# A gated mix of linear attention and a GLU block: the denominators' loads on another issuing queue, and the first weights of the second half loaded in pieces

## The chip, the cores and the metric

The kernel runs on one core of one Trainium2 chip. The metric is the time of one execution on the device, in microseconds (us), measured without the profiler. Beside these times there is one execution recorded by the hardware profiler: its trace gives the start and the length of every instruction on every engine, and of every DMA. The engines are TensorE (PE: matmuls; PEld: its weight loads), VectorE (DVE), ScalarE (ACT), GpSimd (POOL) and SyncE (SP). The last two issue DMAs in this kernel, each in the order of its own queue.

## The reference

The input is x with 2048 tokens (S) of 640 numbers (D), all in float32. There are two branches and a gate between them:

```python
q, k, v = split_heads(x @ wqkv)                   # 32 heads of 20
phi = lambda t: where(t > 0, t + 1, exp(t)) + 1e-6
pq, pk = phi(q), phi(k)
kv  = einsum("bhsd,bhse->bhde", pk, v)
z   = einsum("bhsd->bhd", pk)
num = einsum("bhqd,bhde->bhqe", pq, kv)
den = einsum("bhqd,bhd->bhq", pq, z)[..., None] + 1e-6
a   = merge_heads(num / den) @ wo
b   = (sigmoid(x @ w_gate) * (x @ w_up)) @ w_down   # F = 1536
g   = sigmoid((x * gate_w).sum(-1))
out = g * a + (1 - g) * b
```

The change touches `den`, the denominators: for each token and head, 20 products of `pq` with `z`, summed up; and the weights of the first GLU block (`w_gate`, `w_up`) in the second half of the tokens.

## The kernel before

**Matmuls.** Every product in float32 is computed as three matmuls of rounded parts (high by high, high by low, low by high; `mm3`, lines 404, 405 and 406, so a group of matmuls has one of these three lines in the profile). The large products use a scheme with seven block products in place of eight; class `Block` holds it, with steps `s1` to `s7`. Its operands are linear combinations of weight blocks (the *forms*, three per block: `wg`, `wu` and `ws`; they are computed once, stored to DRAM, and loaded again for the second half by `load_form`, line 1210) and of token blocks. Accumulators in PSUM are called `ch`, `cc`, `dd` and `rot`; VectorE and ScalarE read them (`c<-cc`, `tb<-rot`, `dd<-ch`) before TensorE may write on into the bank. In the profile the names mean: `hf` the gated product h and its rounding parts, `tb` the sum of the down projection, `mr` and `mt` the linear combinations of token sums on their way from and to DRAM (`m_dram`, `mp_dram`), `qe` and `qr` the values of phi(q), stored to `p_dram`.

**Stages.** The tokens lie in four groups of 512, and these in two pairs. The kernel first computes k, v and the sums, then for pair 1 (groups 2 and 3) the queries (`q_phase(1)`), then its 12 GLU blocks with the down projection (`f_phase(1)`, up to about 397 us), then the same for pair 0 (groups 0 and 1): `q_phase(0)`, about 409 to 444 us, and `f_phase(0)`, from about 434 to about 650 us, and at the end the attention's output and the mix. So "the second pair" in time is pair 0.

**q_phase (line 1942)** runs two blocks, A (query rows 2 and 3 of the five) and B (rows 0 and 1), and one plain row between, by a written list `steps`. Its last entries differ between the pairs. When A passes steps 2, 6 and 7 in pair 0, `load_form` is called for forms of the first blocks: after (A, 6) form 1, `wu`, of GLU block 0, and after (A, 7) its form 2, `ws` (2 by 1152 numbers on each of 128 partitions, 1152 KB). A `ws` tile has one of two buffers, and the load waits until the buffer's last reader is done.

**The denominators (`queue_dens`, line 1397)** are queued twice in `f_phase(0)`: at GLU block 3 for groups 2 and 3, at block 7 for groups 0 and 1. For each group they go in this order:

1. `load`: five tiles `pden` (128 partitions by 512, 256 KB) are loaded from `p_dram`. There are four buffers ("t" tiles, shared with `qe` and `qr`): the loads of u = 0 and 1 of both groups go out first, and each further load when `one` has read the buffer before it.
2. `one`: VectorE multiplies a tile by a column of z (`zcol`) and adds it to `fac`. The first has one form (line 432, with `zeps`), the other four another (line 425).
3. `den_dram[:, g] <- fac`, a store on GpSimd's queue.
4. `turn_in`: four loads of 64 KB bring it back turned, `fac <- den_dram`, and one more brings `gs`, the gate.
5. `factor`: VectorE adds the four quarters, takes the reciprocal, multiplies with the gate; the result is stored to `fac_dram` by GpSimd.
6. `turn_out`: four loads `fac <- fac_dram` on SP's queue.

**Queues.** `sp` and `gp` are thin wrappers (`Ring`, with the one `dma_start` at line 361 that all DMA rows of the profile name) around SP's and GpSimd's queues. An issuing instruction waits in its queue until its tile is free, and those behind it wait with it. On SP's queue go most loads, on GpSimd's queue the stores and some loads.

**The planner.** VectorE's and ScalarE's work is not placed by hand. Class `Order` (lines 36 to 301) keeps estimated clocks of TensorE, VectorE and ScalarE while the program is written out, and sets each queued piece of work between the matmuls where the estimate has room and its data are due. It also estimates when a DMA lands (`order.when`), with an issue cost and a lag for each queue (SP: 0.38 and 1.5; GpSimd: 0.55 and 2.2, in the planner's microseconds). So a DMA that changes its queue can also change the static order of the instructions on VectorE and ScalarE.

Of the kernel before, what the change touches and what calls it, by code (L numbers as in the profile page):

```python
# [14 lines left out]
P = 128  # L15
# [352 lines left out]
def v_cost(w):  # L368
    return 0.07 + w / 960

@with_exitstack
def gated_mix_kernel(ctx: ExitStack, tc: tile.TileContext, xt, xn, wk, wv, wo, wst_q, wst_f, out_t):
# [8 lines left out]
    sp, gp = Ring(nc.sync, order, rings, 0, 0.38, 1.5), Ring(nc.gpsimd, order, rings, 1, 0.55, 2.2)  # L381

    def f32(ap):
        return ap.bitcast(F32)
# [34 lines left out]
    def vec2(out, a, b, op, after=""):  # L419
        order.on_vec(width(out), after, 1.0, out, a, b)  # L420
        nc.vector.tensor_tensor(out, a, b, op=op)  # L421

    def vec3(out, a, scalar, b, op0, op1, after=""):
        order.on_vec(width(out), after, 1.0, out, a, b)
        nc.vector.scalar_tensor_tensor(out, a, scalar, b, op0=op0, op1=op1)

    def vec1(out, a, s0, s1=None, op0=OP.mult, op1=None, after=""):
        order.on_vec(width(out), after, 1.0, out, a)
        if op1 is None:
            nc.vector.tensor_scalar(out, a, s0, None, op0=op0)  # L430
        else:
            nc.vector.tensor_scalar(out, a, s0, s1, op0=op0, op1=op1)
# [10 lines left out]
    def add(out, a, b, after=""):  # L443
        vec2(out, a, b, OP.add, after)
# [10 lines left out]
    fac = common.tile([P, NG, TG], F32, name="fac")  # L455
    p_dram = dram.tile([P, KC, NG, TG], F32, name="p_dram")
# [260 lines left out]
    w_dram = {}  # L717
# [249 lines left out]
    c0 = chunks[0]  # L967
# [51 lines left out]
    g = GTBatch(0, [0])  # L1019
# [8 lines left out]
    for c in range(1, 4):  # L1028
        ck = chunks[c]
        if c == 1:  # L1030
# [14 lines left out]
            g = GTBatch(c, batches[c])  # L1045
# [59 lines left out]
        if c == 3:  # L1105
# [19 lines left out]
            def put(n, i, t):  # L1125
                WT[n, i] = t
                W[n, i] = [t[:, c] for c in range(2)]
# [15 lines left out]
        if c > 1:  # L1143
            g = GTBatch(c, batches[c])
# [50 lines left out]
    def tt(name, dt=F32, shape=(P, TG)):  # L1195
        return pw.tile(list(shape), dt, name=name, tag="t", bufs=4)
# [12 lines left out]

    def load_form(n, i):  # L1210
        t = (wg_tile, wu_tile, ws_tile)[i]()
        sp.dma_start(f32(t), w_dram[n[::2] + (i,)])
        put(n, i, t)

    entries = [("q", 1, 0)] + [("f", 1, f) for f in range(FC)]
# [136 lines left out]
    def phi_q(g, u, src, after="p"):  # L1352

        e = tt("qe")
        act(e, src, AF.Exp, after)
        r = src if after == "v" else tt("qr")
        act(r, src, AF.Relu)

        def rest():
            vec3(e, e, 1.0, r, OP.min, OP.add)  # L1360
            gp.dma_start(p_dram[:, u, g], e)
        order.need("phi")
        order.follow(v_cost(TG), rest, "phi")
# [33 lines left out]
    def queue_dens(*gs2):  # L1397

        st = {}

        def load(g, u):
            if u < KC:
                st[g, u] = tt("pden")
                sp.dma_start(st[g, u], p_dram[:, u, g])
                st["at", g, u] = lambda: order.when(st[g, u])

        def one(g, u):
            td = fac[:, g]
            if u == 0:
                vec1(td, st[g, u], zcol[:, 0:1], zeps[:, 0:1], OP.mult, OP.add)  # L1410
            else:
                vec3(td, st[g, u], zcol[:, u:u + 1], td, OP.mult, OP.add)
            load(g, u + 2)
            if u == KC - 1:
                gp.dma_start(den_dram[:, g], td)
                st["at", g, u + 1] = lambda: order.when(den_dram[:, g])

        def turn_in(g):
            for j in range(4):
                js = slice(j * H, (j + 1) * H)  # L1420
                sp.dma_start(fac[js, g].rearrange("h (d c) -> h d c", c=P),
                                  den_dram[:, g, j * P:(j + 1) * P].rearrange("(d h) c -> h d c", h=H))
            st[g, "gs"] = tt("gs")[:, :P]
            sp.dma_start(st[g, "gs"], gate_rep[4 * g:4 * g + 4].rearrange("i h c -> (i h) c"))
            st["at", g, KC + 1] = lambda: max(order.when(fac[:, g]), order.when(st[g, "gs"]))

        def factor(g):
            td = fac[:, g]
            q = td[:, :P]
            add(td[:, :2 * P], td[:, :2 * P], td[:, 2 * P:])  # L1430
            add(q, q, td[:, P:2 * P])
            order.on_vec(5 * P, "")
            nc.vector.reciprocal(q, q)
            vec2(q, q, st[g, "gs"], OP.mult)
            gp.dma_start(fac_dram[:, g], q)
            st["at", g, KC + 2] = lambda: order.when(fac_dram[:, g])

        def turn_out(g):
            for d in range(4):
                sp.dma_start(fac[d * H:(d + 1) * H, g].rearrange("h (j c) -> h j c", c=P),  # L1440
                                  fac_dram[:, g].rearrange("(j h) c -> h j c", h=H))
        order.add(0, 0, lambda: [load(g, u) for u in range(2) for g in gs2], chain=True)
        for u in range(KC):
            for g in gs2:
                order.add(0, v_cost(TG), lambda g=g, u=u: one(g, u), None, lambda g=g, u=u: st["at", g, u](), chain=True)
        for n, (v, fn) in enumerate(((0, turn_in), (2.0, factor), (0, turn_out))):
            for g in gs2:
                order.add(0, v, lambda g=g, fn=fn: fn(g), ("fac", g) if n == 2 else None,
                          lambda g=g, n=n: st["at", g, KC + n](), chain=True)
# [492 lines left out]
    def q_phase(pr, b12, extra):  # L1942

        A, B = (Block(("q", pr, u)) for u in (2, 0))
        steps = [(A, 1), (A, 2)]
        steps += [(4, b) for b in range(2)]
        steps += [(B, 1), (B, 2), (A, 3), (A, 4)]
        steps += ([(A, 5), (A, 6), (A, 7), (B, 3), (B, 4), (B, 5)] if pr else
                  [(B, 3), (A, 5), (B, 4), (A, 6), (B, 5), (A, 7)]) + [(B, 6), (B, 7)]
        order.slack(True)  # L1950
        late = None
        for j, (u, b) in enumerate(steps):
            if isinstance(u, Block):
                blk, s = u, b
                if pr and u is B:
                    for k, key in ((1, ("wg", B.n)), (3, ("w", B.n, 0)), (4, ("w", B.n, 1))):
                        if s == k:
                            order.need(key)
                if s > 1:
                    order.need((nx[1], s if s < 7 else 2))  # L1960
                else:
                    order.need((nx[1], 2))
                getattr(blk, f"s{s}")()
                v = blk.n[2]
                if s == 3:
                    phi_q(2 * pr, v, blk.c11, "v")
                elif s == 6:
                    phi_q(2 * pr + 1, v + 1, blk.c22, "v")
                    phi_q(2 * pr, v + 1, blk.ch)
                elif s == 7 and blk is A:  # L1970
                    late = (2 * pr + 1, v, blk.c12, "v")
                elif s == 7 and pr:
                    phi_q(2 * pr + 1, v, blk.c12, "v")
                if late and blk is B:
                    phi_q(*late)
                    late = None
                if pr:
                    if blk is A and s == 2:
                        queue_g(B.n)
                        queue_s(B.n, 0, 1)  # L1980
                        queue_both(nx, 3)
                        queue_s(B.n, 1)
                    elif blk is A and s == 3:
                        queue_g(("f", pr, 0))
                    elif blk is A and s == 6:
                        load_w()
                    elif blk is A and s == 7:
                        queue_s(("f", pr, 0))
                else:
                    n = {2: ((A, "q", 0, 0), (B, "f", 1, 0)), 6: ((A, "f", 0, 1), (B, "f", 1, 1)),  # L1990
                         7: ((A, "f", 0, 2), (B, "f", 1, 2))}
                    for k, kind, f, i in n.get(s, ()):
                        if k is blk:
                            load_form((kind, 0, f), i)
            else:
                order.need((nx[1], "plain" if b else 2))
                q_unit(pr, u, b, b12)
                if b and not pr:
                    load_form(("f", 0, 0), 0)
            for fn in extra.get(j, ()):  # L2000
                fn()
            order.fill()
            if not pr and u is B and b > 4:
                yield
        if not pr:
            phi_q(2 * pr + 1, 0, B.c12, "v")
        order.slack(False)
# [599 lines left out]
```

## Time and profile before

| | us |
|---|---|
| times of three executions | 733.25, 735.68, 734.04 |
| their median | 734.04 |
| the profiled execution | 734.86 |
| its span, first to last instruction | 733.0 |
| TensorE busy in the span | 726.5 (99%) |
| VectorE busy | 561.6 (77%) |
| ScalarE busy | 355.4 (48%) |
| GpSimd busy | 94.5 (13%) |

How to read the rows that follow. In the *timeline* a row gives the start in us from the start of the span, the length, the engine, the line of the kernel, the operation, the written and the read tile, the shape, and how many such instructions in a row; brackets hold the engine's idle time just before it and what ended that. A DMA row on SPq or POOL is the issuing instruction, and its length there may contain the time that it waited. A row "DMA to landing" gives the times from issue to landing of a group of DMAs (least, median, largest). A row of the *windows* view begins with a stretch A:B, its length, and then the busy time and the number of instructions of the engines PE, PEld, DVE, ACT and POOL (where one engine was asked for, of that engine alone), the granted clock of TensorE as a share of full speed, the mean share of the DMA engines that was busy, and the GB/s moved. In the *waits* a row names an instruction that waited, what it waited for, and three numbers: the sum of the waiting, the count, and the longest. The *chain* follows the work that ended last back to the start; its rows give start, length and what it was.

### The profile page before, as it was taken

What the parts mean: (1) busy time and instruction counts of PE and PEld (TensorE: products, weight loads), DVE (VectorE), ACT (ScalarE), POOL (GpSimd) and SP (SyncE); (2) the same over time, 40 slices, a digit from 0 to 9 for tenths busy, and PEclk for the clock granted to TensorE, in tenths of its full rate; (3) what the DMA queues carried; (4) which work ended last, traced back from release to release, by engine and by line L of the source; (5) the groups of instructions that cost most, each with busy time, mean ns of one, the idle gap of its engine ahead of it and who ended that gap; (6) DMA issues with size and microseconds to landing.
All of it is one profiled execution on the core that took longest, in us unless ns stands there. A gap on an engine that the chain in (4) does not pass through costs nothing.

```text
span 733.0 us, 10098 instructions
## 1 busy us (share of the span) xinstructions
PE 726.5 (99%) x3575; PEld 622.3 (85%) x3575; DVE 561.6 (77%) x987; ACT 355.4 (48%) x661; POOL 94.5 (13%) x161
## 2 busy tenths in 40 slices
PE   9999999999999999999999999999999999999998
PEld 7999999988788888888888888887888888888886
DVE  4978777987677889898989942546685867699976
ACT  5765648358557653535355364453423232332541
POOL 0211111113211211211211211001000041000000
PEclk9999999999999999999999999999999999999999
DMA  8564648697877866557687558888889697859212
GB/s 262 133 195 109 187 120 248 149 343 272 299 276 259 330 239 234 190 213 256 256 328 265 215 175 300 305 244 297 272 278 345 196 335 207 308 209 371 81 68 102
DMA packets 71001, 173.54 MB, mean 237 GB/s; under 512 B 11642, under 2 KB 32394, under 8 KB 67238
## 3 DMA queue, kind: packets, MB, share of 16 engines
q1 hardware_dynamic: 54582, 109.99, 45.8%
q0 software_dynamic: 16224, 62.74, 24.0%
q8 instruction: 28, 0.46, 0.2%
q14 instruction: 23, 0.19, 0.1%
q10 hardware_dynamic: 144, 0.16, 0.1%
HBM read 103.96 MB, written 63.92 MB: 229 GB/s over the span
## 4 chain that ended last, share of the span: by engine, by line
PE 93%; DMA 2%; issue 2%; DVE 1%; ACT 1%; POOL 1%; SPq 0%; POOLq 0%; DVEq 0%; ACTq 0%
PE ch L404 10%; PE ch L406 10%; PE ch L405 10%; PE cc L404 8%; PE cc L406 8%; PE cc L405 8%; PE dd L404 7%; PE dd L405 7%; PE dd L406 7%; PE rot L404 6%; PE rot L405 6%; PE rot L406 6%; DMA pden<-p_dram 1%; DMA p_dram<-qe 1%; PE rot L1521 1%
## 5 line engine op out<-in xcount | busy, mean ns | idle before, releaser
L417 ACT ACTIVATE c<-ch 128x512 f32<-128x512 f32 x52 | 31.0, 597 | 88.1 <-PE ch L406 87.9
L421 DVE TENSOR_TENSOR hf<-c,hf 128x512 fp32r<-128x512 f32 x75 | 51.1, 687 | 25.9 <-ACT hf L417 25.5
L421 DVE TENSOR_TENSOR c<-cc,c 128x512 f32<-128x512 f32 x40 | 27.6, 690 | 40.7 <-PE cc L406 27.9
L417 ACT ACTIVATE hf<-c 128x512 fp32r<-128x512 f32 x75 | 46.0, 624 | 25.4 <-DVE c L421 25.4
L404 PE MATMUL ch<-xth,ws 128*128 128x512 f32 x112 | 43.9, 392 | 0.0
L405 PE MATMUL ch<-xtl,ws 128*128 128x512 f32 x112 | 43.6, 389 | 0.0
L406 PE MATMUL ch<-xth,ws 128*128 128x512 f32 x112 | 43.6, 389 | 0.0
L421 DVE TENSOR_TENSOR tb<-rot,tb 128x512 f32<-128x512 f32 (+1 forms) x61 | 39.3, 674 | 3.0 <-PE rot L406 3.0
L421 DVE TENSOR_TENSOR tb<-dd,tb 128x512 f32<-128x512 f32 x44 | 30.2, 686 | 8.7 <-PE dd L406 8.7
L404 PE MATMUL dd<-xrh,wg 128*128 128x512 f32 x90 | 35.2, 391 | 0.0
L406 PE MATMUL dd<-xrh,wg 128*128 128x512 f32 x90 | 35.0, 389 | 0.0
L405 PE MATMUL dd<-xrl,wg 128*128 128x512 f32 x90 | 35.0, 389 | 0.0
L417 ACT ACTIVATE c<-dd 128x512 f32<-128x512 f32 x22 | 13.2, 598 | 43.3 <-PE dd L406 43.3
L421 DVE TENSOR_TENSOR c<-c,c 128x512 f32<-128x512 f32 x46 | 31.6, 688 | 2.6 <-ACT c L417 2.0
L404 PE MATMUL cc<-xbh,ws 128*128 128x512 f32 x84 | 32.7, 389 | 0.0
L405 PE MATMUL cc<-xbl,ws 128*128 128x512 f32 x84 | 32.7, 389 | 0.0
L406 PE MATMUL cc<-xbh,ws 128*128 128x512 f32 x84 | 32.7, 389 | 0.0
L417 ACT ACTIVATE dd<-ch 128x512 f32<-128x512 f32 x22 | 12.8, 582 | 33.6 <-PE ch L406 33.6
L421 DVE TENSOR_TENSOR wst<-wst 128x256 f32<-128x256 f32 (+2 forms) x69 | 27.4, 413 | 1.5
L404 PE MATMUL rot<-pkh,xnh 128*128 128x320 f32 x90 | 28.0, 312 | 0.1
L405 PE MATMUL rot<-pkl,xnh 128*128 128x320 f32 x90 | 27.8, 309 | 0.0
L406 PE MATMUL rot<-pkh,xnl 128*128 128x320 f32 x90 | 27.8, 309 | 0.0
(648 smaller groups left out, 2325.7 us busy)
## 6 DMA issues: line engine op xcount, KB each, us to landing
wf<-ws POOLq DMA_DIRECT2D x12, 1152.0 KB, 7.6
ws<-wf SPq DMA_DIRECT2D x12, 1152.0 KB, 7.0
wst<-wst_f SPq DMA_DIRECT2D x12, 640.0 KB, 5.2
wf<-wg POOLq DMA_DIRECT2D x12, 640.0 KB, 6.4
wd<-wd POOLq DMA_DIRECT2D x12, 640.0 KB, 7.9
wg<-wf SPq DMA_DIRECT2D x12, 640.0 KB, 6.7
wf<-wd SPq DMA_DIRECT2D x10, 640.0 KB, 10.4
xnst<-xn SPq DMA_DIRECT2D x16, 320.0 KB, 4.2
```

What stands on the lines that cost most here:

```text
L404: nc.tensor.matmul(out, l_hi, r_hi, start=first, stop=False, skip_group_check=True)
L405: nc.tensor.matmul(out, l_hi, r_lo, start=False, stop=False, skip_group_check=True)
L406: nc.tensor.matmul(out, l_lo, r_hi, start=False, stop=last, skip_group_check=True)
L417: nc.scalar.activation(out, src, fn, **kw)
L421: nc.vector.tensor_tensor(out, a, b, op=op)
L1521: nc.tensor.matmul(ps[:w, :w], v[:, m, :w], gt[:, m, c0:c0 + w], start=(m == 0), stop=(m == KC - 1))
```

## The change

There are three edits.

1. The five `pden` loads of each group are issued by GpSimd's queue and not by SP's.
2. The four turning loads `fac <- den_dram` of each group are issued by GpSimd's queue and not by SP's.
3. For GLU block 0 of pair 0, form 2 (`ws`) is loaded in four pieces of columns, in the order 0 to 255, 896 to 1151, 640 to 895, 256 to 639; and in `q_phase(0)` the steps of the blocks A and B stand in another order: A's steps 5, 6 and 7 come each a place or two sooner, B's steps 3, 4 and 5 correspondingly later. The calls of `load_form` that hang on A's steps 6 and 7 move with them.

No arithmetic is added or removed.

```diff
     def load_form(n, i):
         t = (wg_tile, wu_tile, ws_tile)[i]()
-        sp.dma_start(f32(t), w_dram[n[::2] + (i,)])
+        w = t.shape[2]
+        for c0, c1 in ((0, 2 * P), (7 * P, w), (5 * P, 7 * P), (2 * P, 5 * P)) if n == ("f", 0, 0) and i == 2 else ((0, w),):
+            sp.dma_start(f32(t[:, :, c0:c1]), w_dram[n[::2] + (i,)][:, :, c0:c1])
         put(n, i, t)
...
         def load(g, u):
             if u < KC:
                 st[g, u] = tt("pden")
-                sp.dma_start(st[g, u], p_dram[:, u, g])
+                gp.dma_start(st[g, u], p_dram[:, u, g])
                 st["at", g, u] = lambda: order.when(st[g, u])
...
         def turn_in(g):
             for j in range(4):
                 js = slice(j * H, (j + 1) * H)
-                sp.dma_start(fac[js, g].rearrange("h (d c) -> h d c", c=P),
+                gp.dma_start(fac[js, g].rearrange("h (d c) -> h d c", c=P),
                                   den_dram[:, g, j * P:(j + 1) * P].rearrange("(d h) c -> h d c", h=H))
...
         steps += ([(A, 5), (A, 6), (A, 7), (B, 3), (B, 4), (B, 5)] if pr else
-                  [(B, 3), (A, 5), (B, 4), (A, 6), (B, 5), (A, 7)]) + [(B, 6), (B, 7)]
+                  [(A, 5), (B, 3), (A, 6), (A, 7), (B, 4), (B, 5)]) + [(B, 6), (B, 7)]
```

## Prediction

> **What bounds the kernel now.** I read the page first, then TensorE's waits, then the chain of work around the one wait that remains, and last the rows of VectorE and of the two issuing queues there. The times shown are 733.25, 735.68 and 734.04 us; the profiled execution took 734.86 us, 0.82 above their median, with a span of 733.0.
>
> ```profile
> span 733.0 us, 10098 instructions
> PE 726.5 (99%) x3575; PEld 622.3 (85%) x3575; DVE 561.6 (77%) x987; ACT 355.4 (48%) x661; POOL 94.5 (13%) x161
> ...
> PE 93%; DMA 2%; issue 2%; DVE 1%; ACT 1%; POOL 1%; SPq 0%; POOLq 0%; DVEq 0%; ACTq 0%
> ```
>
> TensorE is busy 99% of the span, so a change that adds and removes no matmul can win only what TensorE idles. After the first 400 us (from where the change acts) there is one idle time:
>
> ```profile
> PE rot L404 <- DVE tb L421: 1.4, 1, 1.4
> ```
>
> It stands in the timeline of TensorE, where a 512-column matmul follows the one before by 0.23 us:
>
> ```profile
> 494.57 0.39 PE L406 MATMUL rot<-hf,wf 128*128 128x512 f32 x1
> ...
> 496.61 0.39 PE L406 MATMUL dd<-hf,wf 128*128 128x512 f32 x1
> 498.41 0.50 PE L404 MATMUL rot<-hf,wf 128*128 128x512 f32 x1 [1.41 <-DVE tb L421]
> 498.75 0.39 PE L405 MATMUL rot<-hf,wf 128*128 128x512 f32 x1
> ```
>
> From 496.61 to 498.41 is 1.80 instead of 0.23: 1.57 us lost, and the restart costs 0.34 instead of 0.23: 0.11. The matmul writes on into a `rot` bank that VectorE must first read. The bank was complete about 494.6 to 495 (row 494.57), but VectorE came to it at 497.67:
>
> ```profile
> 480.71 0.69 DVE L421 TENSOR_TENSOR c<-cc,c 128x512 f32<-128x512 f32 x1 [2.89 <-PE cc L406]
> 483.27 0.69 DVE L421 TENSOR_TENSOR hf<-c,hf 128x512 fp32r<-128x512 f32 x1 [1.87 <-ACT hf L417]
> 486.56 1.29 DVE L421 TENSOR_TENSOR hf<-c,hf 128x512 fp32r<-128x512 f32 x2
> 490.03 1.21 DVE L432 TENSOR_SCALAR fac<-pden,zcol,zeps 128x512 f32<-128x512 f32 x2 [2.18 <-DMA pden<-p_dram]
> 491.44 1.42 DVE L425 SCALAR_TENSOR_TENSOR fac<-pden,zcol,fac 128x512 f32<-128x512 f32 x2 [0.20 <-DMA pden<-p_dram]
> ...
> 492.77 0.82 DVE L421 TENSOR_TENSOR mt<-mr,mt 128x640 fp32r<-128x640 f32 x1
> ...
> 497.00 0.75 DVE L425 SCALAR_TENSOR_TENSOR fac<-pden,zcol,fac 128x512 f32<-128x512 f32 x1 [0.61 <-DMA pden<-p_dram]
> 497.67 1.28 DVE L421 TENSOR_TENSOR tb<-rot,tb 128x512 f32<-128x512 f32 x2
> ```
>
> VectorE ran dry before 490.03 (2.18 us, for the first load of the denominators, `pden`) and before 497.00 (0.61). The chain names the same loads:
>
> ```profile
> 484.55 6.78 DMA pden<-p_dram
> ...
> 492.88 4.03 DMA pden<-p_dram
> ```
>
> They are late because of where they stand in SP's queue: behind the weights and the four pieces of `mr`, issued at 481.20, while GpSimd's queue has issued nothing since 448.15 (in the last row, 450 to 480, POOL is the fifth engine: 0.00 (x0)):
>
> ```profile
> 481.20 2.17 SPq L361 DMA_DIRECT2D mr<-m_dram  x4
> 483.54 9.65 SPq L361 DMA_DIRECT2D pden<-p_dram  x8
> 448.15 0.54 POOL L361 DMA_DIRECT2D p_dram<-qe  x1 [4.41 <-DVE qe L425]
> 450.00:480.00 30.00, 30.00 (x134) 24.86 (x133) 12.16 (x19) 9.65 (x17) 0.00 (x0) 1.00 0.72 264
> ```
>
> **Part 1, the `pden` loads on GpSimd's queue.** Twenty loads of 256 KB change queue; an issue costs GpSimd 0.54 (row 448.15) instead of SP's third of a microsecond. In the built program they follow the ten stores `p_dram<-qe` directly, so the first four (there are four buffers) leave soon after those stores have landed, some 30 us before they are used. With that the planner also sets VectorE's first two denominator steps earlier: behind the step of 480.71, before the `hf` of 483.27. I lay VectorE's new order on the rows. The first pair takes 1.21 and ends at about 482.5. `hf` stays at 483.27. The second pair takes 1.42 and ends at 485.3. The two `hf` of 486.56 end at 487.85. Then stand the third and fourth pairs, `mt`, one `c`, the fifth pair, and then the `tb` that TensorE waits for. Each load from the third pair on needs a buffer that VectorE has just left, so all depends on the time L from issue to landing on GpSimd's queue. These rows bound it: first all twenty `pden` loads on SP; then the GpSimd stores of the same size issued while 1152 KB of weights are in flight (438 to 449 us); last the `pden` loads of 489.5 to 494.
>
> ```profile
> DMA to landing us min/median/max: 2.6/4.6/8.0
> DMA to landing us min/median/max: 4.6/5.6/6.6
> DMA to landing us min/median/max: 2.6/2.9/3.3
> ```
>
> So L lies between 2.6 and 8.0. I take 5.6, from the same queue and size beside the same weight load. The last load of the third pair has its buffer at 482.5 and lands at 488.1, before it is wanted; VectorE ends that pair at 487.85 + 1.42 = 489.3. The fourth pair's buffers are free at about 484.6 and 485.3, so it lands at 490.2 and 490.9 and is done at 491.65. The fifth pair's last load starts there, lands at 494.9, and is used by 494.9 + 0.75 = 495.65. TensorE resumed 0.74 after its `tb` began (498.41 less 497.67), and would have gone on at 496.84 (496.61 + 0.23): a `tb` that begins by 496.10 costs no wait, and 495.65 does. So up to L = 6.05 the whole stall goes: 1.57 + 0.11 = 1.68 us. Above that both landings count: the `tb` begins at 482.5 + L + 0.75 + L + 0.75, so 484.0 + 2L, and equals the old 497.67 at L = 6.84. At 8.0 it begins at 500.0, 2.33 us worse than now.
>
> [...]
>
> What GpSimd delays: behind its waiting `pden` loads stand only stores of `mt` and of the denominators. What comes late next is the chain of `mr`, `mt` and its store, since ScalarE waits in it, in order, before freeing a `ch` bank:
>
> ```profile
> 508.26 0.74 ACT L417 ACTIVATE mt<-mr 128x640 fp32r<-128x640 f32 x1 [2.80 <-DMA mr<-m_dram]
> 508.91 0.58 ACT L417 ACTIVATE c<-ch 128x512 f32<-128x512 f32 x1
> ...
> 510.11 0.39 PE L404 MATMUL ch<-xth,ws 128*128 128x512 f32 x1
> ```
>
> TensorE reaches that bank at 510.11, and at 508.5 once the stall is gone; the bank is free at 508.91 + 0.58 = 509.5. `mt` would have to start about 1 us sooner. In VectorE's new order the first `mt` comes at 491.65 instead of 492.77, and the second waits for the `tb` steps, which come 2 us earlier (495.65 against 497.67). So I expect 1.1 to 2 us, and no new wait; if the chain did not move, 1.0 of the 1.68 would come back here.
>
> **Part 2, the turning.** Sixteen loads of 64 KB from `den_dram` also go to GpSimd. SP held them for long:
>
> ```profile
> 514.82 9.63 SPq L361 DMA_DIRECT2D fac<-den_dram  x4
> ```
>
> The weights queued behind them come up to those 9.6 us earlier, and no matmul waited for them: worth nothing. The factors that follow move up on VectorE, between the steps of 517.1 and 521.7. One factor fills 1.97 us (first row); the place has 4.61 - 0.69 = 3.92 free (second), and two need 3.94:
>
> ```profile
> 534.18:536.15 1.97, 1.87 (x5) 1.00 0.99 414
> 517.09:521.70 4.61, 0.69 (x1) 1.00 1.04 386
> ```
>
> So that costs nothing; without that cover up to 3.9 us of VectorE would stand before the next `c`. The stores behind the turning wait for VectorE anyway. `mt<-m_dram` and the like, 16 issues, go back by some 25 us behind the second factors; they have until 697.5:
>
> ```profile
> L421 DVE TENSOR_TENSOR mt<-mt x5: 284/419/425, 697.5 to 700.1; 128x256 f32<-128x256 f32 x4, 128x128 f32<-128x128 f32 x1
> ```
>
> **Part 3, the pieces of `ws` and the order of steps.** The diff also puts the second product block's third step behind the first block's fifth. The same matmuls run, the first block ends 4.9 us sooner and its `ws` buffer with it, so the load issued at 437.86 starts at about 433; three issues of 0.32 us are added. TensorE takes the load's first columns at 443.79, and it landed 5.4 us after its issue, at 443.26. It was in time by 0.5 us; earlier is worth nothing in this execution. One restart goes, 0.32 instead of 0.23, since that `ch` bank is now free long before:
>
> ```profile
> 437.86 0.32 SPq L361 DMA_DIRECT2D ws<-wf  x1
> DMA to landing us min/median/max: 5.4/5.4/5.4
> 434.15 0.48 PE L404 MATMUL ch<-xah,wg 128*128 128x512 f32 x1
> 434.47 0.39 PE L405 MATMUL ch<-xal,wg 128*128 128x512 f32 x1
> 443.79 0.39 PE L404 MATMUL ch<-xth,ws 128*128 128x512 f32 x1
> ```
>
> Added waits here: the fifth and sixth steps add onto a bank that ScalarE has just read, but a 1.36 us step of the other block now stands between, so I count 0; the reads take 0.6.
>
> **Sum.** 1.68 + 0.10 = 1.78 us of the profiled 734.86: 733.1. Taken from the median instead, 732.3. I forecast **732.5 us**, nearer to the median, which is what gets measured. A measurement of this kernel can tell about 0.3% from no change, 2.2 us; the whole gain that the profile offers is below that.
>
> **Rivals.** (a) *GpSimd's loads come late* (slower). L over 6.84, in both pairs that wait for a landing. For it: SP's own `pden` loads reached 8.0, and the second round falls into a stretch with as much traffic. Against it: 2.9 is the median once the weights have landed. At 8.0 the first round loses 2.33. In the second round a denominator step stands ahead of a `tb` of 563.38; its buffer is free one step of 0.54 after the `c` of 555.88, at about 557.1; the load lands at 565.1, and with 0.75 and the two `hf` (1.29) the `tb` begins at 567.1 and ends at 567.8, where TensorE wants the bank at 567.26:
>
> ```profile
> 555.88 0.69 DVE L421 TENSOR_TENSOR c<-cc,c 128x512 f32<-128x512 f32 x1 [2.95 <-PE cc L406]
> ...
> 563.38 0.69 DVE L421 TENSOR_TENSOR tb<-dd,tb 128x512 f32<-128x512 f32 x1 [0.92 <-PE dd L406]
> 567.26 0.39 PE L404 MATMUL dd<-hf,wf 128*128 128x512 f32 x1
> ```
>
> That is 0.6 more: 734.0 + 2.9 = **736.9 us**. (b) *Nothing is won*: L near 6.8, or the `mt` chain takes the place of the wait: 734.0 us, between 733.4 and 736. [...] (c) *More is won*: the executions without a profile lose more than this one, for instance where the `ws` of 437.86 lands over 0.5 us later; they spread over 2.4 us. Some 3 us less, **731.2 us**.
>
> **How the numbers follow.** The forecast, 0.47: 731.9 to 733.4 (the profiled base of 733.1 and 0.3 for the `mt` chain). (b) 0.14, (a) 0.22, (c) 0.17. Faster by over 0.3% (under 731.8) is (c), 0.17; slower (over 736.2) is (a), 0.22; the rest, 0.61, lies within. The range goes from 731.0, just beyond (c), to 736.9, the worst bound of L.
>
> **What would show it.** Right: no wait of TensorE for `tb` near 497; first `pden` issues on GpSimd at 449 to 455; the first denominator step at about 481.3; `ws` in four pieces from about 433. Wrong: a wait for `tb` that remains or grows, with VectorE idle for `pden` just before it (L over 6); a wait for the `ch` bank near 508 with ScalarE idle for `mr`; a wait for `dd` near 567; TensorE idle in the reordered block, 426 to 440. The forecast fails if landings on GpSimd's queue are much slower than its stores were.

## The result

The changed kernel takes **735.65 us** in the median of 20 executions (734.75 to 737.53), the kernel before 734.02 (733.25 to 737.2, 20 executions). The ratio, which compares all executions and not the two medians, is 1.0016 with a 95% interval of 1.0010 to 1.0023: 1.2 us slower (0.7 to 1.7). That is clear of zero and inside the 2.2 us that the prediction set as the bound of "the same". The time lies in the range of 731.0 to 736.9, but the forecast of 732.5 had the wrong sign.

The profiled execution of the changed kernel took 734.77 us, among the shortest of its 20. First its page and its waits of TensorE between 420 and 690 us (sum, count, longest):

```profile
span 733.0 us, 10118 instructions
PE 726.8 (99%) x3575; PEld 622.9 (85%) x3575; DVE 561.7 (77%) x987; ACT 355.1 (48%) x661; POOL 113.9 (16%) x197
...
PE rot L404 <- DVE tb L421: 1.0, 1, 1.0
```

The busy time is the same within 0.3 us, and one wait of TensorE for `tb` is still there. It is another one. Near 497 TensorE now goes through; the wait is near 567, in the second round of the denominators. The timeline of TensorE, of VectorE, and of GpSimd's queue there, and the landing of the four loads issued from 555.9 to 559.3:

```profile
567.12 0.40 PE L406 MATMUL cc<-hf,wf 128*128 128x512 f32 x1
568.49 0.47 PE L404 MATMUL rot<-hf,wf 128*128 128x512 f32 x1 [0.97 <-DVE tb L421]
...
555.09 0.99 DVE L432 TENSOR_SCALAR fac<-pden,zcol,zeps 128x512 f32<-128x512 f32 x2
...
562.74 0.75 DVE L425 SCALAR_TENSOR_TENSOR fac<-pden,zcol,fac 128x512 f32<-128x512 f32 x1 [2.53 <-DMA pden<-p_dram]
...
566.40 0.74 DVE L425 SCALAR_TENSOR_TENSOR fac<-pden,zcol,fac 128x512 f32<-128x512 f32 x1
...
567.67 0.68 DVE L421 TENSOR_TENSOR tb<-rot,tb 128x512 f32<-128x512 f32 x1
...
555.92 1.06 POOL L361 DMA_DIRECT2D pden<-p_dram  x2 [15.41 <-DVE fac L432]
...
DMA to landing us min/median/max: 5.9/6.3/7.5
```

The loads of the third step leave at 555.92, as soon as VectorE has left their buffers (the row of 555.09). They land after 5.9 to 7.5 us. VectorE, whose next instruction in its fixed order needs the first of them, stands 2.53 us until 562.74. Behind that step stand two `hf`, three `tb`, another denominator step (566.40), one `c`, and only then the `tb<-rot` of 567.67 that frees TensorE's bank. TensorE goes on at 568.49 where 567.35 was possible: 1.14 us, and 0.19 for restarts around it. Before, these denominator steps came behind the `tb` steps, from 569.14 on (TensorE's use of the bank, then VectorE):

```profile
568.62 0.39 PE L404 MATMUL rot<-hf,wf 128*128 128x512 f32 x1
...
567.34 1.28 DVE L421 TENSOR_TENSOR tb<-rot,tb 128x512 f32<-128x512 f32 x2
...
569.14 0.54 DVE L432 TENSOR_SCALAR fac<-pden,zcol,zeps 128x512 f32<-128x512 f32 x1
```

Where the first round ran, one new wait of TensorE, for weights (`wf`), appeared. The matmul before it and the one that waited (0.47 apart instead of 0.23), and the landing of the three `wf` loads issued from 505.5 to 506.9, of which two are on record:

```profile
518.27 0.39 PE L406 MATMUL ch<-xth,ws 128*128 128x512 f32 x1
518.74 0.50 PE L404 MATMUL dd<-hf,wf 128*128 128x512 f32 x1
...
L361 SPq DMA_DIRECT2D wf<-wd x3: 662/681/716, 505.5 to 506.9; - x3
DMA to landing us min/median/max: 13.2/13.7/14.2
```

The first of them landed 13.2 us after 505.45, at 518.69, just before that matmul.

### The profile page after: what moved, and what is told of

Read it like the earlier page. It is cut to its first block, busy times and chain, and to the rows that moved or that the text cites. A ratio compares the mean times of both kernels' runs of the same rounds, so it can differ in the third digit from the quotient of the medians.

```text
span 733.0 us, 10118 instructions
## 1 busy us (share of the span) xinstructions
PE 726.8 (99%) x3575; PEld 622.9 (85%) x3575; DVE 561.7 (77%) x987; ACT 355.1 (48%) x661; POOL 113.9 (16%) x197
## 4 chain that ended last, share of the span: by engine, by line
PE 86%; DMA 6%; issue 3%; DVE 2%; ACT 1%; POOL 1%; SPq 0%; POOLq 0%; ACTq 0%; DVEq 0%
PE ch L404 9%; PE ch L405 9%; PE ch L406 9%; PE cc L404 7%; PE cc L405 7%; PE cc L406 7%; PE dd L404 7%; PE dd L405 7%; PE dd L406 7%; PE rot L404 6%; PE rot L405 5%; PE rot L406 5%; DMA wf<-wd 2%; DMA pden<-p_dram 2%; DMA ws<-wf 2%
```

## The experiments

Each compares with the kernel before, executed in turn with it on the same chip; the chips of 1 to 4, 5 to 8, 9 to 12 and 13 to 15 differ, so each series has its own median of before. All of them compute the whole output. "Lost" below is always the same measure: TensorE's 512-column matmuls follow one another by 0.23 us, and what a pair is further apart than that is lost time. In the profiled executions of the kernel before and of the changed kernel, the time less all that is lost after 400 us is 733.08 both times (734.86 - 1.78, 734.77 - 1.69); over all kernels below it lies between 732.5 and 733.8. So the lost time, place by place, accounts for the differences between these profiles but for some 1.3 us, which lie in the first 400 us, at the end, or outside the matmuls counted:

| profiled execution | us | 434 | 492-498 | 508 | 517-528 | 531-537 | 566-570 |
|---|---|---|---|---|---|---|---|
| before | 734.86 | 0.10 | 1.68 | | | | |
| before, again (1) | 733.55 | 0.10 | 0.53 | | | | |
| changed | 734.77 | | | | 0.36 | | 1.33 |
| changed, again (5) | 735.41 | | | 0.32 | 0.89 | 0.11 | 1.29 |
| part 1 alone (2) | 737.90 | 0.10 | 1.13 | | 1.79 | 0.07 | 1.16 |
| part 2 alone (6) | 736.04 | 0.10 | 1.93 | 0.11 | | 1.12 | |
| part 3 alone (3) | 734.58 | | 1.14 | | | | |
| parts 2 and 3 (7) | 735.26 | | 1.30 | | | 0.75 | |
| changed, second round's steps later (4) | 736.29 | | 0.51 | 1.37 | 0.92 | 0.52 | |
| changed, second round on SP (8) | 737.53 | | 0.18 | 1.27 | 0.88 | 0.50 | |
| first round alone (9) | 736.64 | 0.10 | 0.44 | | 1.94 | | |
| second round alone (10) | 736.97 | 0.10 | 0.82 | | | | 2.31 |
| first round, turning later (11) | 733.21 | 0.10 | | | | | |
| the same, again (15) | 734.40 | 0.10 | | | | 0.48 | |
| the same, turning on GpSimd (13) | 740.08 | 0.10 | | | 7.04 | | |
| the same, with part 3 (14) | 736.14 | | 2.44 | | 0.82 | 0.37 | |
| 11 with parts 2 and 3 (12) | 742.06 | | 0.93 | | 8.01 | | |

Two of them lost more elsewhere (8: 1.28 at 675; 9: 0.80 at 596). One profile is one execution out of many; medians and intervals stand with each experiment.

**1. The kernel before, again.**

> The kernel before, unchanged, once more, to see whether the wait of TensorE for tb near 497 us (1.57 us, and 0.11 for the restart) belongs to every execution. Theory A (the profiled execution lay 0.8 us above the median because it alone had the full wait, so the changed kernel had little to win): an execution near 733.3 to 734.0 us with a wait near 497 of under 0.8 us. Rival B (the wait is in every execution, and the 0.8 us lie elsewhere): a wait of 1.4 to 1.7 us again, whatever the time.

It took 733.55 us with 0.53 lost near 497 instead of 1.68. So A holds in its numbers: the wait is always at this place (all six profiles with the first round's `pden` on SP have it, 0.53 to 1.93, 1.2 on average), but its size varies from execution to execution, and the profile on which the prediction worked had a larger one than the average. It was not alone in that, as A had it: kernel 6 lost 1.93. Medians of 734.0 to 735.1 for the kernel before are 1 to 2 us above 733.0.

**2. Part 1 alone**, and **3. part 3 alone** (its two hunks of the diff above).

```diff
-                sp.dma_start(st[g, u], p_dram[:, u, g])
+                gp.dma_start(st[g, u], p_dram[:, u, g])
```

> The kernel before with the pden loads alone on GpSimd's queue (part 1). Theory A (the loss is the second round of denominators: its third step stands ahead of tb on VectorE and waits for a load issued at about 556): 735.2 to 735.8 us, a wait of TensorE for tb near 567 of 1 us or more, none near 497. Rival B (the first weights and the reordered steps cost the time): 732.5 to 734 us. Rival C (the turning on GpSimd's queue costs it): 732.5 to 734 us.

> The kernel before with the four pieces of the first ws and the reordered steps alone (part 3). Theory A (part 1 makes the loss): 733.9 to 734.2 us, TensorE without a pause from 426 to 444 us. Rival B (this part makes it): 735 to 736 us, with a pause there or with later loads that land later. Rival D (it wins what executions without a profile lose at the first ws): 733.0 to 733.5 us.

Part 1: 736.46 us against 735.05 of before; ratio 1.0012 (0.9997 to 1.0028), and its shortest execution, 735.93, is 2.4 us above the shortest of before. The wait near 567 is there (1.16), but it isn't the only one: 1.79 are lost for `ws` and `wf` at 518 to 522, and 1.13 at 493 to 498, where none was expected. Part 3: 735.51 us, ratio 1.0003 (0.9982 to 1.0023), shortest 733.71 against 733.57: no difference that can be measured, and the restart of 0.10 at 434 is gone.

**4. The changed kernel with the second round's steps later.**

```diff
-                st["at", g, u] = lambda: order.when(st[g, u])
+                st["at", g, u] = lambda: order.when(st[g, u]) + (6.0 if gs2[0] == 0 and u > 1 else 0.0)
```

> The changed kernel, with the due time of the denominators' third to fifth steps set 6 us later in the second round alone, so that VectorE comes to the tb that TensorE waits for near 567 before any step that waits for a late load. Theory A (VectorE held there by a load): the wait near 567 goes, 733.5 to 734.3 us, 1.3 to 2 us under the changed kernel. Rivals B and C (another part costs the time): 735.2 to 735.8 us, as the changed kernel, the wait near 567 gone or not.

735.36 us, ratio to before 1.0007 (0.9995 to 1.0020). The wait near 567 is gone. Up to 576 the two kernels give VectorE the same instructions in the same order, but for the two denominator steps that stood ahead of `tb<-rot` (562.74 and 566.40 above); so the wait came from these, and not from the queue as such. The rest of A's sum failed: I expected to be back at the time of before or under it, and other waits stand in the first round. The waits of TensorE from 420 to 690 us:

```profile
PE ch L404 <- ACT c L417: 1.1, 1, 1.1
PE dd L404 <- DMA wf<-wd: 0.6, 1, 0.6
PE rot L404 <- DVE tb L421: 0.5, 2, 0.2
```

The first is the chain of `mr` and `mt` at 508; the second is `wf` at 520.

**5. The changed kernel, again**, **6. part 2 alone**, **7. parts 2 and 3**, **8. the changed kernel with the second round's loads on SP.** The edits of 6 and 8:

```diff
-                sp.dma_start(fac[js, g].rearrange("h (d c) -> h d c", c=P),
+                gp.dma_start(fac[js, g].rearrange("h (d c) -> h d c", c=P),
```

```diff
-                gp.dma_start(st[g, u], p_dram[:, u, g])
+                (gp if gs2[0] == 2 else sp).dma_start(st[g, u], p_dram[:, u, g])
```

> The changed kernel, unchanged, once more beside the kernel before on the same chip. Theory A (a load on GpSimd's queue holds VectorE ahead of the tb near 567, in every execution): a wait near 567 of 0.8 to 2.5 us again, a lowest time 1.2 to 1.8 us above the lowest of before. Rival E (the executions merely differ in how late their loads land, and the changed kernel drew worse ones): no steady wait at 567, lowest times of both kernels within 0.4 us.

> The kernel before with the turning loads alone on GpSimd's queue (part 2). By the prediction: the same time as before within 0.3 us. Theory F (the turning held the weights behind it on SP's queue, which costs in executions with late loads): up to 0.5 us faster in the median, lowest time unchanged. Rival C (it delays other loads): 0.5 to 1.5 us slower, with TensorE waiting for ws or wf near 518 to 522.

> The changed kernel with the pden loads put back on SP's queue: parts 2 and 3 without part 1. Theory A (part 1 alone makes the loss): the time of the kernel before within 0.4 us, in the median and the lowest, no wait near 567, the wait near 497 back at 0.4 to 1.7 us. Rival B or C: 1 to 1.8 us above before.

> The changed kernel with the second round's pden loads put back on SP's queue, the first round's on GpSimd's. Theory A (the second round's place is the loss, the first round is a gain or nothing): lowest time as before within 0.3 us, median 0 to 0.8 us below before, no wait near 567, at most 0.5 us near 497. Rival G (the first round costs as well, through the loads that follow it: mr, wf and ws of 505 us): 0.5 us or more above before, with waits between 505 and 522.

Before had a median of 734.75 beside these. The changed kernel: 737.14, ratio 1.0022 (1.0005 to 1.0039), with 1.29 lost near 567 again, though its shortest execution is only 0.8 us above that of before. Part 2: 736.10, ratio 1.0012 (0.9994 to 1.0030). Parts 2 and 3: 736.08, ratio 1.0016 (1.0000 to 1.0033). So theory A in its strict form fell: without part 1 (7) the median stays 1.3 us above before, where 0.4 was allowed, though the interval reaches down to 1.0000. From 5 to 8 only the queue of the second round's loads changes: with those loads on SP's queue the median is 734.99, ratio 0.9999 (0.9984 to 1.0014), and the wait near 567 is gone. The intervals of 5 and 8 overlap a little. G's waits between 505 and 522 are in the profile of 8 (1.27 and 0.88), but not its 0.5 us in the median.

What part 2 does is seen in 6. The four `mr` loads issued at about 511.5 to 513.4 land later, first before, then part 2 alone:

```profile
L361 SPq DMA_DIRECT2D mr<-m_dram x4: 324/421/513, 511.5 to 512.8; - x4
DMA to landing us min/median/max: 12.7/12.7/12.8
```

```profile
L361 SPq DMA_DIRECT2D mr<-m_dram x4: 323/419/432, 512.1 to 513.4; - x4
DMA to landing us min/median/max: 15.4/15.5/15.6
...
528.44 0.74 ACT L417 ACTIVATE mt<-mr 128x640 fp32r<-128x640 f32 x1 [3.10 <-DMA fac<-den_dram]
529.21 0.83 DVE L421 TENSOR_TENSOR mt<-mr,mt 128x640 fp32r<-128x640 f32 x1 [3.34 <-ACT mt L417]
...
533.08 0.50 PE L404 MATMUL rot<-hf,wf 128*128 128x512 f32 x1 [0.23 <-DVE tb L421]
```

`mr` lands 15.5 us after its issue instead of 12.7 (13.6 in the repetition of before, 15.2 in kernel 7, which also has part 2). ScalarE's row names a turning load as what it waited for; but `mt` reads `mr` alone, whose two landings on record, 527.73 and 527.91, come after the turning's last before it, 527.33. ScalarE starts `mt` at 528.44 (525.17 before), VectorE's `mt` at 529.21 (525.94 before) holds the four `tb` and the `c` behind it, and TensorE waits for `tb` at 530 to 533: 1.12 us lost. Each of the waits is small (0.23 us in the last row), but three banks in a row add up.

**9. The first round alone**, **10. the second round alone**, **11. the first round with the turning later**, **12. the changed kernel, mended in both rounds.** 9 and 10 are the kernel before with `gp` in place of `sp` for one round's `pden`, as in the second diff of 5 to 8. 11 is 9 with one line more; 12 is 11 with parts 2 and 3:

```diff
-                st["at", g, u + 1] = lambda: order.when(den_dram[:, g])
+                st["at", g, u + 1] = lambda: order.when(den_dram[:, g]) + (12.0 if gs2[0] == 2 else 0.0)
```

> The kernel before with the pden loads of the first round alone on GpSimd's queue; everything else as before, so the turning stays on SP's queue, and comes there some 10 us sooner. Theory H (the wait near 497 goes, and what is late next takes the gain: mr at 508, the weights of 505 at 518 to 520, which here stand behind the turning): 0 to 1.2 us above before, TensorE without a wait for tb near 497 but with 1 to 2 us between 505 and 522. The prediction's own step (1.68 us are won and nothing is late next): 0.7 to 1.7 us below before.

> The kernel before with the pden loads of the second round alone on GpSimd's queue. Theory A (the third step of that round stands ahead of tb and waits 6 to 7 us for its load): 0.9 to 1.6 us above before in the median, a wait of TensorE for tb near 567 to 570 of 1.0 to 1.3 us, and the wait near 497 as before. Rival E (no price of its own): within 0.4 us of before.

> The first round's pden loads on GpSimd's queue, the turning on SP's as before, but with its due time set 12 us later in the first round, so that it stands behind the weights and mr of 505 us again. Theory H (the gain of the first round is lost to the turning's transfers and to mr and weights that land late): 0.4 to 1.2 us below before, waits between 505 and 522 under 0.6 us in all. Its rival (the weights of 505 us are bound by the DMA engines, turning or not): within 0.5 us of before, with a wait for wf near 518 to 520 of 0.4 to 1 us again.

> The changed kernel with the second round's pden loads back on SP's queue and the first round's turning (on GpSimd's queue) due 12 us later. Theories A and H together (the second round's place and the turning's time are what the changed kernel loses): 0.3 to 1.2 us below before, no wait near 567, less than 0.6 us in all between 505 and 533. If the turning on GpSimd's queue costs wherever it stands (the transfers share the engines with mr): 0.5 to 1.3 us above before, with waits of TensorE for tb near 530 to 533.

Before: 734.80. The second round alone: 737.04, ratio 1.0033 (1.0021 to 1.0045), and 2.31 lost from 566 to 570, more than A expected, since there all three banks in turn waited. The first round alone: 736.36, ratio 1.0018 (1.0004 to 1.0032): the wait near 497 is smaller, and 1.94 us are lost for weights that stand behind the turning on SP's queue. The first round with the turning later: **733.60, ratio 0.9981 (0.9972 to 0.9990)**, 1.2 us below before, and in its profile no wait of TensorE after 434. No other kernel came so near to the 1.68 that the prediction had worked out for part 1. The later due time keeps the turning's loads behind the weights; the planner also set the four `mr` loads of 506 ahead of `ws` there, so the turning's place is not the only thing that differs from 9. 12, where the same turning is on GpSimd's queue, is the slowest: 738.38, ratio 1.0058 (1.0039 to 1.0078). Expected was a gain, or at worst 1.3 us.

**13 to 15. One thing changed against kernel 11.** 13 adds part 2 (the turning on GpSimd's queue), 14 adds part 3, 15 is kernel 11 itself. The planner's order on VectorE and ScalarE is the same in 13 as in 15 up to about 526 us, so before that only the turning's queue and place differ.

> The kernel that has no wait after 434 us (first round's pden loads on GpSimd's queue, its turning due 12 us later), with one thing changed: the turning loads on GpSimd's queue. Theory J (on SP's queue the turning stands behind the weights of 508 us and one load after the other; on GpSimd's it leaves at once and its transfers delay those weights): 2 to 5 us above that kernel, with a wait of TensorE for ws or wf at 517 to 525. Rival (the queue does not matter, the 3.6 us of the kernel tried before came from part 3's order): within 0.5 us of that kernel.

> The same quiet kernel with part 3 added (ws in four pieces, the reordered steps). The prediction's step: 0.1 us faster (the restart at 434), else nothing. Rival B (part 3 costs): 0.5 us or more slower, with a pause that is not in the quiet kernel.

> The quiet kernel once more, beside the other two: 0.4 to 1.6 us below before, no wait of TensorE after 440 us.

Before: 734.71. Kernel 11 again: 734.40, ratio 0.9988 (0.9973 to 1.0004), with 0.48 lost near 535 that were not expected. With part 3: 734.02, ratio 0.9982 (0.9967 to 0.9998), while its profiled execution was the slowest of its twelve: part 3 costs nothing that can be measured, and what it may win is not resolved. In three comparisons, then, the medians of kernel 11 with or without part 3 lie 0.3 to 1.2 us below before; two of the three intervals exclude no change. With part 2: **738.34, ratio 1.0046 (1.0029 to 1.0063)**. The median moved by 3.9 us for the issuing queue of sixteen loads of 64 KB, eight in each round; the profile loses the time at the first round's eight. The traffic from 508 to 521 us, by queue (q1 is what SP issues, q0 what GpSimd issues; packets, MB, share of the 16 DMA engines), and the landing of the weights; first kernel 11:

```profile
q1 hardware_dynamic: 1084, 3.72, 82.2%
q0 software_dynamic: 196, 0.92, 17.6%
...
ws<-wf SPq DMA_DIRECT2D x1, 1152.0 KB, 6.5
```

Then the same with the turning on GpSimd's queue, with TensorE's waits and one window (PE is the first engine; behind POOL's column stands the granted clock):

```profile
q1 hardware_dynamic: 696, 2.39, 61.7%
q0 software_dynamic: 414, 1.25, 36.0%
...
ws<-wf SPq DMA_DIRECT2D x1, 1152.0 KB, 11.6
...
PE ch L404 <- DMA ws<-wf: 2.9, 1, 2.9
PE dd L404 <- DMA wf<-wd: 0.8, 1, 0.8
...
522.00:530.00 8.00, 7.19 (x22) 5.27 (x20) 2.11 (x4) 4.07 (x8) 0.00 (x0) 0.62 0.94 314
```

GpSimd's queue took 36.0% of the engines' time instead of 17.6%, SP's 61.7% instead of 82.2%. The `ws` of 508.3 to 508.8 landed 11.6 us after its issue instead of 6.5, and TensorE, which wants it at 517.2, lost 7.04 us from there on. On SP's queue the turning's loads left from 511.3 on, behind the weights; on GpSimd's they left at 507.7 to 511.5, beside them, and landed 8.7 us after their issue in the median. The shares also show that the 16 engines were full in both kernels (99.8% and 97.7% from the two queues), but moved 4.66 MB in kernel 11 and 3.66 in 13, from 508 to 521 us: GpSimd's queue took 18 points more of their time for 0.33 MB more. Why these loads cost the engines so much is not shown.

## Why the prediction was wrong

Two terms of the prediction's sum failed. It counted nothing for the second round, which lost 1.33 us, and it counted the first round's 1.68 us as won in full, where the runs show less.

**What was there to win.** The prediction subtracted the stalls of one execution, 1.78 us. The place and the cause were right (the loads of `pden` behind the weights on SP's queue), but the profiled execution had a large stall: another lost 0.63 in all. Less the 733.0 that is left, the median of before holds about 1.0 us of it; this is an estimate, since what is left varies by 1.3 us over the profiles. The times shown already pointed there, since the profiled time lay 0.82 above the median; I moved the base most of the way to the median and left the 1.78 whole.

**Part 1, first round: right in the two profiles of the changed kernel, and in part by luck.** The first loads left GpSimd at 448.57 (449 to 455 was said), the first denominator step came at 481.21 (481.3), and the wait near 497 is gone from both profiles of the changed kernel. The landing times were not one number L: the loads issued while the weights were in flight took 6.2 to 7.1 us, those after it 3.1. With the first alone, 484.0 + 2L would have given 498; the sum of two different ones gave a `tb` at 495.10 (495.65 was said). But the L of 5.6 was too small, and with it goes the 1.68. In the eleven profiles with the first round on GpSimd's queue, the third pair's loads took 6.9 to 10.6 us (8.0 was the prediction's bound), and six of the eleven lost 0.18 to 2.44 us at 492 to 498 again; two of these, kernels 4 and 8, run the changed kernel's instructions up to there. The largest loss is in the profile of kernel 14, with these four loads and VectorE's wait for them:

```profile
L361 POOL DMA_DIRECT2D pden<-p_dram x4: 539/539/539, 481.6 to 485.0; - x4
DMA to landing us min/median/max: 9.0/9.7/10.6
...
492.13 2.76 DVE L425 SCALAR_TENSOR_TENSOR fac<-pden,zcol,fac 128x512 f32<-128x512 f32 x4 [4.82 <-DMA pden<-p_dram]
```

On average the eleven lost 0.5 us there, and the six with this round on SP's queue 1.2. So the move is worth about 0.7 us, an estimate from one profile of each run.

**What is late next: wrong in size and in place.** For the chain of `mr` and `mt` I named 1.0 us at 508 as what might come back, and counted 0.3. It was 0 and 0.32 in the two profiles of the changed kernel, 1.27 in 8 and 1.37 in 4. Not named at all was `wf` at 518 to 520: TensorE wants it 1.8 us sooner than before (518.50 instead of 520.31), and though the three loads leave 1.7 to 1.8 us sooner, the first, for which it waits, lands at 518.69. Before, that landing is not on record; in kernels 3 and 7, with `pden` on SP's queue, the load left at 506.62 and 506.81 and landed at 516.44 and 515.62. So TensorE came sooner and the load came later too: 0.36 to 0.92 lost in the profiles of the changed kernel, 4 and 8.

**Part 1, second round: the step that failed.** The prediction's sum counts nothing for it, and rival (a) 0.6 us at L = 8.0, because it followed the `tb` that frees `dd` (wanted at 567.26). The bank that waits is `rot`, freed by the `tb<-rot` a few steps further on. In the kernel before, that bank was free at 568.08 (567.34 and 0.74) for a matmul at 568.62. In the changed kernel TensorE wanted it at 567.35, and VectorE had been given two denominator steps (0.75 and 0.74) and a wait of 2.53 ahead of it. With 6.8 us from issue to use (555.92 to 562.74), not 8.0, that is 1.33 us. It is in each of the kernels that have the second round on GpSimd's queue with the planner's own due times (1.16 to 2.31), and in none of the others.

**Part 2: "worth nothing" was wrong where it could be measured.** I looked at who waits behind the turning on SP's queue, and not at whom the turning overtakes when it leaves that queue. On kernel 11, 3.9 us; alone, 1.3 us by the medians and 0.9 by the ratio (-0.4 to 2.2), which the interval doesn't separate from nothing. In the changed kernel the turning runs at 500.7 to 505, beside the weights of 503 to 507, and `wf` landed 13.2 to 14.2 us after its issue. How much of the 0.36 and 0.89 lost there is the turning's, and how much comes from the other loads that moved, no run separates.

**Part 3: right.** The pieces are issued from 432.99 (433 was said), the restart is gone, and nothing else can be measured.

**The sum**, by these terms on the profiled execution: 1.78 won as predicted, but 0.36 at 518 and 1.33 at 567 given back: -0.09, and 734.77 against 734.86 is -0.09. The two sides agree so closely by luck, given the 1.3 us that this measure leaves open between profiles. The median of the changed kernel holds about 2.6 us of lost time (735.65 - 733.1), the profile 1.69 and its repetition 2.61. Which of the places is larger in the slower executions stays open, since the times without a profile do not tell. Rival (a) had the right mechanism and side, loads on GpSimd's queue that VectorE waits for; its condition (L over 6.84 in both landings) was not needed: in the second round one late landing was enough.

## What to carry to other kernels

When a stall is removed, ask first what else is due within the next tens of us, since TensorE comes to all of it sooner (here to `wf` by 1.8 us, with 1.68 of stall and 0.10 of restart removed). The turning loads that moved to another queue did not only get free of what stood ahead of them; they also stopped yielding to it: the `ws` of 508 us landed 11.6 us after its issue in kernel 13, 6.5 in kernel 11. So the loads that a moved load now runs beside are those to check. And before a stall of one profile is counted as gain, or as gone, see in a second execution whether it is always so.

## What the runs showed of the hardware beyond that

The longest waits of TensorE cost more than their length. In kernel 13, after 3.1 us without a matmul, the granted clock was 0.62 on average from 522 to 530 (the window above; 0.50 from 522 to 526), and matmuls followed one another by 0.43 instead of 0.23 us:

```profile
520.34 0.50 PE L404 MATMUL ch<-xth,ws 128*128 128x512 f32 x1 [2.94 <-DMA ws<-wf]
...
524.40 0.63 PE L406 MATMUL dd<-hf,wf 128*128 128x512 f32 x1
524.83 0.63 PE L404 MATMUL rot<-hf,wf 128*128 128x512 f32 x1
...
528.15 0.40 PE L406 MATMUL dd<-hf,wf 128*128 128x512 f32 x1
528.38 0.40 PE L404 MATMUL cc<-xth,ws 128*128 128x512 f32 x1
```

The slow pace began 0.8 us after the restart and lasted to about 528, and it cost some 2.6 us of the 7.04 (the wait and its restart took 3.21, a second wait 1.21). Kernel 12 shows the same after 4.0 us: a granted clock of 0.57 from 522 to 530, and 0.43 us from matmul to matmul. Waits of up to 1.8 us after 400 us in the other kernels were not followed by it (the longest, in kernel 6: a clock of 1.00 from 485 to 500 and from 500 to 515). No run has a wait of a length between 1.8 and 3.1 us after 400 us.
